# Decode through two attention and two MLP layers: unread products, two load sizes and a ring position at the end of layer 0

## The chip, the core and the metric

The kernel runs on one core of a Trainium2 chip. The metric is device time in microseconds (us) from the start of the program to its end; the profile's span is the time from the first to the last instruction. TensorE is called PE, VectorE DVE, ScalarE ACT, SyncE SP.

## The reference

Four sequences, one token each, width D = 640. Two layers with the same weights and the same caches: an attention over the last 1024 positions of 32 heads of 128, and a gated MLP of width 1728. All is float32.

```
x = x + A(layernorm(x));  x = x + B(layernorm(x))      # twice
A: q = x @ wq                        # [4, 32 heads, 128]
   p = softmax(q . k[..., -1024:, :] * 128**-0.5)
   return (p . v[..., -1024:, :]) @ wo
B: gate = x @ W_gate;  up = x @ W_up
   return (gate * (gate > 0) * up) @ W_down
```

K and V differ for each sequence and head, so each value of the caches is used for one product, and 312 MB are read from HBM in all.

## The kernel before

The heads are worked in 8 groups of 4. One DRAM tensor `stream` [128, columns] holds, in the order of use, for each group g its W_q (2560 columns), K (16384), the next group's W_q, V (16384) and W_o (2560), and behind the groups the MLP's weights: the left-over gate and up columns (1920), three gate and up blocks (5120 each), the left-over of W_down (960) and three blocks of W_down (2560 each). A column is 128 x 4 bytes.

All of it goes through one SBUF tile `store` of 55,040 columns. A list `todo` (lines 80 to 113) names the loads in order, each with its layer, its range, its largest size and, where given, its place. `load()` (line 119) takes the head of the list, places it at the cursor (`state["at"]`) or at its given place, goes back to the base when a piece no longer fits, and issues it on SP if none of its columns is live. `done()` (line 154) is called behind each product in the program's order; it frees the columns just used and calls `load()`. So a load waits on SP for the product that frees its last column, and all loads behind it wait on the same queue.

At the end of layer 0 the front of `store` is kept: layer 1 begins with group 7, whose W_q, K, V and W_o stay, together with the end of group 6's V and its W_o. What is left for streaming then is a ring of RING = 6912 columns from the column KEPT on. Through it go all MLP weights of layer 0 and, from its base again (the second `todo.append([KEPT])`, line 102), W_q of group 6 for layer 1 and the first 4096 columns of its K. After that the places of group 7's K and V come free as layer 1 uses them.

On PE each attention group is: `scores` (line 268, products `ps`, L273) with the projection of the group before after its first head, `softmax` (line 277: maximum on DVE, exponential on ACT), the next group's query, `totals` and `turned` (sums, and 8 transposes of the probabilities), and `values` (line 304: 8 blocks of 4 heads, products `po`, L309). For the last group of layer 0 there is no next query; there `table(AF.Sqrt)` loads ACT's table. The weights of V's blocks come in loads of 4096 columns (two blocks), then 2048, 1024 and 1024.

`warm()` (line 235) is a product of the identity with some tile into a PSUM buffer that nobody reads. `waits` (line 302) says after which block and head of V, in the last group of layer 0, how many of these stand: 5, 5, 2, 1 and 1, each 256 columns wide. More of them, 128 wide, stand in layer 0's MLP, `forward` (line 369): behind each fifth of the second and third gate blocks (line 385) and behind each row block of W_down's first two blocks (line 417).

`forward` computes on PE: the left-over gate columns (`gate(3)`, 15 products of 128 columns), then blocks 0, 1, 2 (20 products of 256 columns each), then `down(3)`, `down(0)`, `down(1)`, `down(2)`.

Of the kernel before, what the change touches and what calls it, by code (L numbers as in the profile page):

```python
# [12 lines left out]
B, D, H, DH, W, F = 4, 640, 32, 128, 1024, 1728  # L13
P = 128
# [9 lines left out]
WQ, KV, WO = KC * GH * P, GH * 4096, GH * D  # L24


GU0, GU = KC * 3 * P, KC * 4 * 256
WD0 = GU0 + 3 * GU
TAIL, WD1, WD = WD0 + D, WD0 + D + 2 * QUARTER, 4 * D
# [3 lines left out]
AT = {}  # L33
# [21 lines left out]
M0 = AT["mlp"]  # L55
# [12 lines left out]
def decode_kernel(ctx: ExitStack, tc: tile.TileContext, x, stream, sel, out):  # L68
# [13 lines left out]
    def run(layer, lo, hi, most=LONG, place=None):  # L82
        todo.append((layer, lo, hi, place, most))

    def steps(layer, lo, *sizes, place=None):
        for n in sizes:
            run(layer, lo, lo + n, n, place)
            lo += n
            place = None if place is None else place + n
# [8 lines left out]
    run(0, vsplit, AT["k", 7], place=0)  # L98
    steps(0, AT["k", 7], *[4096] * 7, 2048, 1024, 1024, 1280, 1280, place=FRONT + WQ)
    todo.append([KEPT])  # L100
    steps(0, M0, GU0, *[1536] * 10, WD1 - WD0, 2 * D, 3 * D, 3 * D, 2 * D, D, D)
    todo.append([KEPT])
    run(1, AT["q", 6], AT["q", 6] + WQ)
    steps(1, AT["k", 6], 2048, 2048)
    todo.append([FRONT, 0])
    steps(1, AT["k", 6] + 4096, 2560, 2048, 2048, 2048, 3584)
# [124 lines left out]
    def table(func):  # L231
        t = small.tile([P, 1], F32, name="t", bufs=1)
        nc.scalar.activation(t, eps_sb, func)

    def warm(moving=None):

        m = ident if moving is None else moving
        t = ps_p.tile([P, 512], F32, tag="p", name="unread")
        nc.tensor.matmul(t[:, :m.shape[-1]], ident, m, start=True, stop=True)  # L239
# [45 lines left out]
    def totals(sums):  # L285
        nc.tensor.matmul(ms[:, :GH * B].rearrange("p (h b) -> p h b", b=B), sums.to_broadcast([P, P]), ident_hb,  # L286
                         start=True, stop=True)
        r = small.tile([P, GH * B], F32, name="r")
        nc.vector.reciprocal(r, ms[:, :GH * B])
        return r  # L290
# [7 lines left out]
            nc.vector.tensor_copy(t[:, 4 * j:4 * j + 4], pp.rearrange("p c (b r) -> p c r b", r=32)[:, :, :GH, :])  # L298
        return t


    waits = {(1, 3): 5, (3, 3): 5, (5, 3): 2, (6, 3): 1, (7, 1): 1}

    def values(layer, g, t, last):

        for c in range(8):
            for h in range(GH):
                lo = AT["v", g] + (c * GH + h) * 512
                nc.tensor.matmul(po[32 * h:32 * h + B], t[:, c, h], get(layer, lo, 512),  # L309
                                 start=c == 0, stop=c == 7, tile_position=(0, 32 * h))  # L310
                done(layer, lo, 512)
                if last and (c, h) in waits:
                    for _ in range(waits[c, h]):
                        warm(probs[:, :256])
        nc.scalar.copy(gates, po)  # L315
        if last:
            warm(probs[:, :256])
# [18 lines left out]
    def attention(layer, gs):  # L336
        load()
        xT, d = normalized()
        rs = []
        query(layer, gs[0], xT, lambda: rs.append(deviation(d)))  # L340
        rstd = rs[0]
        table(AF.Exp)
        query_out(rstd)
        query_turned()
        before = None
        for g, after in zip(gs, gs[1:] + [None]):
            scores(layer, g, 0)
            if before is None:
                go_on()
            else:  # L350
                project(layer, before, values_turned(r), False)
            for h in range(1, GH):
                scores(layer, g, h)
            sums = softmax()
            if after is not None:
                query(layer, after, xT)
                query_out(rstd)
            else:
                table(AF.Sqrt)
            r = totals(sums)  # L360
            t = turned()
            if after is not None:
                query_turned()
            values(layer, g, t, layer == 0 and after is None)
            before = g
        project(layer, before, values_turned(r), True)


    def forward(layer):
# [38 lines left out]
        def down(j, last=False):  # L408
            for f in range(4 if j < 3 else 1):
                lo = M0 + (WD1 + j * WD + f * D if j < 3 else WD0)  # L410
                w = get(layer, lo, D)
                for g in range(4):
                    nc.tensor.matmul(y[32 * g:32 * g + B], hTs[j][:, f], w[:, g * QUARTER:(g + 1) * QUARTER],
                                     start=False, stop=last and f == 3, tile_position=(0, 32 * g))
                done(layer, lo, D)
                if layer == 0 and j < 2:
                    warm()
            if j == 3:
                w = get(layer, M0 + TAIL, 2 * QUARTER)
                for g in range(4):  # L420
                    r = slice(64 * (g // 2), 64 * (g // 2) + 64)
                    nc.tensor.matmul(y[32 * g:32 * g + B], hTs[j][r, 1], w[r, g % 2 * QUARTER:(g % 2 + 1) * QUARTER],
                                     start=False, stop=False, tile_position=(r.start, 32 * g))
                done(layer, M0 + TAIL, 2 * QUARTER)
# [80 lines left out]
```

## Time and profile before

| | us |
|---|---|
| three timed runs | 747.44, 747.61, 748.26 |
| median | 747.61 |
| the profiled execution | 748.54 |
| its span | 746.8 |
| PE busy in it | 498.0 (67%) |
| DVE busy, ACT busy | 59.3, 42.2 |

HBM was read at 418 GB/s over the span. The granted clock of PE is 0.802 of full speed in the mean. A float32 product appears as two PE records. The chain of waits follows the work that ended last back from the end; where it stands on a load, the time counted runs from that load's issue, and loads queue, so it isn't the duration of the transfer. A busy PE is counted by modelled ends of products.

### The profile page before, as it was taken

To read this page: it belongs to the slowest core of one execution; us is meant where nothing else is said; L and a number is where in the kernel's file an instruction comes from. 1 tells how busy PE (TensorE), PEld (TensorE's weight loads), DVE (VectorE), ACT (ScalarE), POOL (GpSimd) and SP (SyncE) were. 2 spreads that over 40 slices of the span, in tenths; PEclk is the share of its full clock that TensorE was granted. 3 is DMA by queue.
4 is the path that set the end of the run, shared out by engine and by line. 5 is a ranking of instruction groups with operands and counts; after the bars stand their busy time and mean duration, and the time that the engine had idled before them with its cause. 6 is when DMAs were issued, how large, how long until landed. Compare 5 with 4: busy or idle time off the path is not lost.

```text
span 746.8 us, 8319 instructions
## 1 busy us (share of the span) xinstructions
PE 498.0 (67%) x3876; PEld 167.6 (22%) x3876; DVE 59.3 (8%) x159; ACT 42.2 (6%) x74; POOL 0.2 (0%) x4
## 2 busy tenths in 40 slices
PE   3467466665855565966988997556665487576595
PEld 1122112212210121311434232111221022222142
DVE  2000100001010010101011110100001000010110
ACT  2000000000000000001001000000000000000100
POOL 0000000000000000000000000000000000000000
PEclk9969787876876776885999897868869778698777
DMA  9999999999999999999989999999999999999996
GB/s 382 454 416 433 436 429 429 436 423 440 425 438 429 437 422 425 442 412 426 374 332 390 411 447 403 412 416 444 430 442 423 442 423 435 428 430 427 412 428 282
DMA packets 14730, 312.99 MB, mean 419 GB/s; under 512 B 1636, under 2 KB 1892, under 8 KB 6120
## 3 DMA queue, kind: packets, MB, share of 16 engines
q1 hardware_dynamic: 14544, 312.37, 98.2%
q8 instruction: 30, 0.49, 0.3%
q10 hardware_dynamic: 152, 0.09, 0.0%
q14 instruction: 4, 0.03, 0.0%
HBM read 312.37 MB, written 0.08 MB: 418 GB/s over the span
## 4 chain that ended last, share of the span: by engine, by line
DMA 71%; PE 25%; another core or an unknown queue 2%; DVE 1%; ACT 1%; issue 1%; SPq 0%; ACTq 0%; DVEq 0%
DMA store<-in_stream 71%; PE ps L273 7%; PE po L309 7%; PE yy L332 3%; PE ms L321 2%; PE unread L239 1%; PE qp L253 1%; PE pp L297 1%; PE qp L381 1%; PE po L381 1%; PE ms L264 1%; DVE nm L280 0%; ACT probs L282 0%; SPq L144 0%
## 5 line engine op out<-in xcount | busy, mean ns | idle before, releaser
L273 PE MATMUL ps<-store,qz 128*4 128x512 f32 x1024 | 168.6, 719 | 100.9 <-DMA store<-in_stream 100.4
L309 PE MATMUL po<-store,pT 128*4 128x512 f32 x1024 | 165.1, 752 | 71.5 <-DMA store<-in_stream 71.5
L273 PEld LDWEIGHTS ps<-store,qz 128*4 128x4 f32 x1024 | 30.4, 97 | 208.6 <-issue 111.7
L309 PEld LDWEIGHTS po<-store,pT 128*4 128x4 f32 x1024 | 29.1, 98 | 185.5 <-issue 104.2
L253 PE MATMUL qp<-store,xT 128*4 128x512 f32 x160 | 39.3, 721 | 27.8 <-DMA store<-in_stream 27.6
L282 ACT ACTIVATE probs<-ps,nm 128x1024 f32<-128x1024 f32 x16 | 17.8, 1113 | 316.7 <-DVE nm L280 316.7
L280 DVE TENSOR_REDUCE nm<-ps 128x1 f32<-128x1024 f32 x16 | 19.6, 1225 | 196.5 <-PE ps L273 196.5
L332 PE MATMUL yy<-store,oT 128*4 128x160 f32 x512 | 27.6, 372 | 4.3 <-DVE oT L324 4.3
L324 DVE TENSOR_TENSOR oT<-ms,r 128x16 f32<-128x16 f32 x16 | 2.8, 175 | 345.7 <-PE ms L321 345.7
L315 ACT COPY gates<-po 128x512 f32<-128x512 f32 x16 | 9.4, 585 | 308.0 <-PE po L309 308.0
L321 PEld LDWEIGHTS ms<-sel_sb,gates 128*128 128x128 f32 x128 | 20.5, 244 | 20.2 <-issue 18.0
L321 PE MATMUL ms<-sel_sb,gates 128*128 128x4 f32 x128 | 21.9, 295 | 0.9 <-ACT gates L315 0.8
L297 PE MATMUL pp<-sel_sb,probs 128*128 128x128 f32 x128 | 20.9, 317 | 0.0
L381 PE MATMUL po<-store,xT 128*4 128x256 f32 x160 | 15.9, 495 | 7.0 <-DMA store<-in_stream 7.0
L297 PEld LDWEIGHTS pp<-sel_sb,probs 128*128 128x128 f32 x128 | 18.6, 178 | 0.0
L286 PE MATMUL ms<-sel_sb,sm 128*128 128x16 f32 x32 | 7.4, 308 | 15.8 <-ACT probs L282 15.7
L264 PEld LDWEIGHTS ms<-sel_sb,gates 128*128 128x128 f32 x128 | 16.8, 204 | 4.5 <-DVE gates L258 4.4
L264 PE MATMUL ms<-sel_sb,gates 128*128 128x4 f32 x128 | 16.6, 253 | 1.7 <-DVE gates L258 1.7
L253 PEld LDWEIGHTS qp<-store,xT 128*4 128x4 f32 x160 | 6.0, 93 | 50.3 <-DMA store<-in_stream 31.3
L332 PEld LDWEIGHTS yy<-store,oT 128*4 128x4 f32 x512 | 13.8, 100 | 12.1 <-DVE oT L324 5.7
L258 DVE TENSOR_SCALAR gates<-qp,rstd 128x512 f32<-128x512 f32 x16 | 12.0, 750 | 41.1 <-PE qp L253 39.8
L286 PEld LDWEIGHTS ms<-sel_sb,sm 128*128 128x128 f32 x32 | 5.8, 226 | 34.6 <-ACT probs L282 28.1
(62 smaller groups left out, 128.1 us busy)
## 6 DMA issues: line engine op xcount, KB each, us to landing
store<-in_stream SPq DMA_DIRECT2D x26, 6656.0 KB, 49.5
store<-in_stream SPq DMA_DIRECT2D x11, 2048.0 KB, 29.6
store<-in_stream SPq DMA_DIRECT2D x2, 6784.0 KB, 50.2
store<-in_stream SPq DMA_DIRECT2D x7, 1280.0 KB, 10.9
store<-in_stream SPq DMA_DIRECT2D x10, 768.0 KB, 7.1
store<-in_stream SPq DMA_DIRECT2D x7, 1024.0 KB, 8.2
store<-in_stream SPq DMA_DIRECT2D x1, 6848.0 KB, 46.8
store<-in_stream SPq DMA_DIRECT2D x1, 6720.0 KB, 46.6
```

The lines of the kernel that those rows point to most:

```text
L253: nc.tensor.matmul(qp[q:q + B], xT[:, c], get(layer, lo, GH * P), start=c < 4, stop=c > 0, tile_position=(0, q))
L258: nc.vector.tensor_scalar(gates, qp, rstd, SCALE, op0=ALU.mult, op1=ALU.mult)
L264: nc.tensor.matmul(ms[:, h * B:h * B + B], gates[:, h * P:(h + 1) * P], sel_b, start=True, stop=True)
L273: nc.tensor.matmul(ps[32 * b:32 * b + GH, j, :], qz[:, turn[0], b, GH * h:GH * h + GH], get(layer, lo, 512), start=h == 0, stop=h == GH - ...
L280: nc.vector.tensor_reduce(nm, flat, axis=AX.X, op=ALU.max, negate=True)
L282: nc.scalar.activation(probs, flat, AF.Exp, bias=nm, accum_out=sums)
L286: nc.tensor.matmul(ms[:, :GH * B].rearrange("p (h b) -> p h b", b=B), sums.to_broadcast([P, P]), ident_hb, start=True, stop=True)
L297: nc.tensor.transpose(pp[:, c, :], probs[:, (4 * j + c) * P:(4 * j + c + 1) * P], ident)
L309: nc.tensor.matmul(po[32 * h:32 * h + B], t[:, c, h], get(layer, lo, 512), start=c == 0, stop=c == 7, tile_position=(0, 32 * h))
L321: nc.tensor.matmul(ms[:, b * GH:b * GH + GH], gates[:, b * P:(b + 1) * P], ident[:, b:P:32], start=True, stop=True)
L332: nc.tensor.matmul(y[32 * q:32 * q + B], oT[:, h], get(layer, lo + q * QUARTER, QUARTER), start=False, stop=last and h == GH - 1, tile_pos ...
L381: nc.tensor.matmul(gu[32 * g:32 * g + B, :2 * n], xT[:, c], get(layer, lo, 2 * n), start=c == 0, stop=c == KC - 1, tile_position=(0, 32 * g))
```

## The change

Five edits, all at the end of layer 0 or just behind it.

1. `waits` and the 14 unread products between the last group's V blocks are taken out; the one behind the last block (line 317) stays.
2. In the same group, between the scores and the sums, two unread products of `gates` (512 columns wide) are put on PE.
3. The first MLP load, 1920 columns, becomes two of 1152 and 768. The ten pieces of 1536 behind it become 1536 x 3, 1024, 768, 1536 x 5 and 1280.
4. The cursor no longer goes back to KEPT before group 6's W_q. It goes on where the last MLP weights end, and W_q is loaded as 512, 1536 and 512 columns instead of 2560 at once.
5. The unread products behind W_down's first block are taken out; those behind its second block stay.

```diff
-    steps(0, M0, GU0, *[1536] * 10, WD1 - WD0, 2 * D, 3 * D, 3 * D, 2 * D, D, D)
-    todo.append([KEPT])
-    run(1, AT["q", 6], AT["q", 6] + WQ)
+    steps(0, M0, 9 * P, 6 * P, *[1536] * 3, 1024, 768, *[1536] * 5, 1280, WD1 - WD0, 2 * D, 3 * D, 3 * D, 2 * D, D, D)
+    steps(1, AT["q", 6], 512, 1536, 512)
...
-    waits = {(1, 3): 5, (3, 3): 5, (5, 3): 2, (6, 3): 1, (7, 1): 1}
...
-                if last and (c, h) in waits:
-                    for _ in range(waits[c, h]):
-                        warm(probs[:, :256])
...
                 table(AF.Sqrt)
+                if layer == 0:
+                    warm(gates)
+                    warm(gates)
...
-                if layer == 0 and j < 2:
+                if layer == 0 and j == 1:
                     warm()
```

## The prediction

> **What bounds the kernel now.** I read the page first: its span and the shares of the chain of waits.
>
> ```profile
> span 746.8 us, 8319 instructions
> ...
> DMA 71%; PE 25%; another core or an unknown queue 2%; DVE 1%; ACT 1%; issue 1%; SPq 0%; ACTq 0%; DVEq 0%
> ```
>
> The stream of loads sets the end; whatever changes the time must change when the loads run. So next I cut the span into stretches around the only place where the change acts, the end of layer 0. Columns: PE, PE weight loads, DVE, ACT and POOL busy time with instruction counts, then granted clock, share of the DMA engines, GB/s.
>
> ```profile
> 343.15:370.00 26.85, 24.07 (x121) 9.25 (x121) 1.93 (x4) 3.27 (x5) 0.00 (x0) 0.76 1.01 418
> 370.00:378.00 8.00, 6.92 (x134) 4.81 (x134) 1.68 (x8) 0.86 (x3) 0.00 (x0) 1.00 0.41 136
> 378.00:394.00 16.00, 12.50 (x114) 4.89 (x114) 0.86 (x4) 0.73 (x2) 0.00 (x0) 1.00 1.02 414
> 394.00:404.00 10.00, 9.27 (x132) 4.48 (x132) 0.61 (x3) 0.39 (x2) 0.00 (x0) 1.00 0.99 368
> 404.00:412.00 8.00, 6.45 (x62) 2.62 (x62) 2.17 (x8) 2.01 (x4) 0.00 (x0) 0.91 1.00 391
> 412.00:441.80 29.80, 28.28 (x250) 9.36 (x250) 3.05 (x7) 1.79 (x3) 0.00 (x0) 0.91 1.04 436
> ```
>
> From 370 to 378 us the loads move 136 GB/s where the stretch before moved 418: the stream runs dry there. Why, the chain in order of time tells (start, length, what; a product of float32 is two records).
>
> ```profile
> 343.18 3.64 PE ps L273 x16
> ...
> 349.42 0.61 PE ms L286 x2
> ...
> 351.82 3.53 PE po L309 x16
> ...
> 358.01 1.83 PE po L309 x16
> ...
> 368.28 0.98 PE po L309 x4
> ...
> 369.34 0.59 ACT gates L315
> ...
> 371.30 1.31 PE yy L332 x32
> ...
> 374.29 1.08 PE qp L381 x25
> ...
> 375.39 4.22 DMA store<-in_stream
> ```
>
> The chain is on PE from 343 to 375 us: the MLP's ring is full, and the next load waits for the first MLP products (L381, which begin at 374.29) to free its columns; it is issued at 375.39. On the way stand the unread products (a group of PE instructions from 351 to 370 us: records, busy us, mean ns):
>
> ```profile
> L239 PE MATMUL unread<-probs,sel_sb 128*128 128x256 f32 x30 | 8.4, 412 | 0.0
> ```
>
> 28 of these 30 records are the 14 products that the change takes out, 7.8 us of PE. Whether that moves anything depends on when V lands. Pairs of rows, the issue of a load (start, length) and its KB and us to landing:
>
> ```profile
> 333.34 0.33 SPq L144 DMA_DIRECT2D store<-in_stream  x1
> ...
> store<-in_stream SPq DMA_DIRECT2D x1, 512.0 KB, 29.6
> ...
> 357.87 0.33 SPq L144 DMA_DIRECT2D store<-in_stream  x1
> ...
> store<-in_stream SPq DMA_DIRECT2D x1, 768.0 KB, 14.3
> ...
> 360.37 0.33 SPq L144 DMA_DIRECT2D store<-in_stream  x1
> ...
> store<-in_stream SPq DMA_DIRECT2D x1, 768.0 KB, 13.6
> ...
> 375.39 0.33 SPq L144 DMA_DIRECT2D store<-in_stream  x1
> ...
> store<-in_stream SPq DMA_DIRECT2D x1, 768.0 KB, 4.2
> ```
>
> Following `load()` through its list gives the loads' order and names. The last 1024 columns of V land at 333.34 + 29.6 = 362.94; the last two MLP pieces that fill the ring at 357.87 + 14.3 = 372.17 and 360.37 + 13.6 = 373.97, so in a full queue 768 KB (1536 columns) are 1.80 us apart. W_o follows V with 2560 columns, 3.0 us at that rate, so by 365.9. The refill lands at 379.59 instead of 373.97 + 1.80 = 375.77. By landings the dry spell costs 3.8 us, and a load into an empty queue pays 4.2 - 1.8 = 2.4 us for starting.
>
> **The change part by part.** *The 14 products.* Without them PE waits for V's last piece, not for itself: 362.94 + 0.98 (the x4 row) = 363.9 against 369.3 now, 5.4 us sooner. W_o is there in time: 369.34 to 371.30 is 1.96 us, so the projection begins at 365.9, when W_o's last piece is landing. The first MLP products move from 374.29 to 368.9, and their weights (landing before 368.5: 372.17 less two pieces of 1.80) are in.
>
> *The first MLP load in two, and the pieces behind it.* The first refill becomes 1024 columns and is freed by eight of the fifteen 128-column products instead of twelve, 0.4 us sooner (1.08 us over the fifteen). Its issue: 375.39 - 5.4 - 0.4 = 369.6. To lose nothing it must be out 2.4 us before 373.97, so by 371.6: it is 2.0 us early. Behind it on SP stand only further loads of the ring, which wait for PE in their order; each then follows the landing of its data by under 1.5 us, while the ring holds 6912 columns, 8.1 us of stream. The dry spell goes: 3.8 us by landings, 8 x (1 - 136/418) = 5.4 us by bytes, since most engines of the sixteen are done before the slowest. PE waits for landings, so I take 4.1, near the lower.
>
> *Four more DMAs in all* (one more in the first load, one in the pieces behind it, two in W_q). Rows bound the price of each between nothing (768 KB in 1.80 us are 437 GB/s, no less than the 436 of the last stretch above, whose loads are larger) and the 2.4 us of an empty queue. I take 0.05 each, the rounding of such rows, 0.2 us in all, because the queue stays full; at the other end stand 9.6. The Trainium skill (DMA: Bandwidth & Descriptors, Anatomy of one DMA) gives every DMA about 2.0 us of fixed cost beside its bytes at 436 GB/s, by which four more would add 8 us. The trace agrees where the queue is dry (768 KB: 3.8 us by its formula as an estimate, 4.2 measured) and not where it is full (1.80).
>
> *Two unread products in the softmax.* Their width is 512; the nearest rows are the 256-wide ones, 412 ns a record, and 512-wide blocks of four tiles, 3.53 us for two at clock 0.50. So 1.8 us each at half clock, 3.5 together, into PE's idle slot from 346.8 to 349.42: up to 1.0 us over. That delays the sums and the transposes, and nothing waits for these: V's blocks 0 and 1 are in, blocks 4 and 5 come only at 357.9 (the landing for which the load of 357.87 waited). If that cover were gone it would cost 1.0. In return PE is busy without a break from 343.2. The clock changes only at the ends of stretches of 3.41 us:
>
> ```profile
> 270.67:274.09 3.42, 1.12 (x10) 0.10 (x3) 0.00 (x0) 0.00 (x0) 0.00 (x0) 0.99 0.87 369
> 274.09:277.50 3.41, 1.23 (x8) 0.26 (x12) 0.00 (x0) 0.00 (x0) 0.00 (x0) 0.50 1.12 482
> ...
> 376.49:379.90 3.41, 1.52 (x24) 0.55 (x16) 0.28 (x1) 0.01 (x1) 0.00 (x0) 1.00 0.89 337
> 379.90:383.31 3.41, 3.41 (x38) 1.53 (x34) 0.42 (x2) 0.37 (x1) 0.00 (x0) 1.00 1.03 428
> ...
> 352.59:356.01 3.42, 3.42 (x18) 0.92 (x11) 0.00 (x0) 0.00 (x0) 0.00 (x0) 0.51 0.98 407
> 356.01:359.42 3.41, 3.41 (x26) 1.74 (x24) 0.00 (x0) 0.00 (x0) 0.00 (x0) 1.00 0.98 402
> ```
>
> A full stretch raises it (356.01), 1.12 busy of 3.42 drops it (274.09), 1.52 of 3.41 keeps it. With the two products the rise comes near 349 instead of 356; V's first four blocks are then done by about 355, and PE stands until 357.9.
>
> *W_q in the ring's end; no unread products in the first block of W_down.* A step of such a product is 381.94 - 381.52 = 0.42 us:
>
> ```profile
> 380.98 0.61 PE L381 MATMUL qp<-store,xT 128*4 128x256 f32 x8
> 381.52 0.49 PE L239 MATMUL unread<-sel_sb 128*128 128x128 f32 x2
> 381.94 0.61 PE L381 MATMUL qp<-store,xT 128*4 128x256 f32 x8
> ...
> 396.50 6.91 DMA store<-in_stream
> ```
>
> Four of them free 1.7 us of PE, and these are covered: the last MLP weights come at 396.50 + 6.91 = 403.4, and PE waits for them; without that cover they would be a gain.
> W_q's 512 columns go out with those weights and 1536 a step of W_down sooner. From 394 to 412 us the stream misses 10 x (1 - 368/414) + 8 x (1 - 391/414) = 1.6 us; these edits gain between 0 and that; I take half, 0.8, since landings lose less than bytes. W_q's and the later pieces wait on SP for products of W_down, with only loads of the next K behind them, whose first reader is some 30 us away.
>
> **Sum.** 4.1 + 0.8 - 0.2 = 4.7 us. The profiled execution took 748.54 us (1.74 around its span), 0.93 above the median; 748.54 - 4.7 = 743.84, and with 0.93 off that is **742.9**. The bounds of the terms together: a gain of 3.6 to 7.0.
>
> **What is late next.** PE then runs layer 1's first group from kept weights while its own releases feed the stream, until the first K of another group goes out:
>
> ```profile
> 428.37 0.33 SPq L144 DMA_DIRECT2D store<-in_stream  x1
> ...
> store<-in_stream SPq DMA_DIRECT2D x1, 256.0 KB, 13.4
> ...
> 436.65 0.33 SPq L144 DMA_DIRECT2D store<-in_stream  x1
> ```
>
> That load leaves at 436.65, and the one before it lands at 428.37 + 13.4 = 441.8: 5.1 us ahead, 2.7 more than the 2.4 it needs. If the stream gains that much more than PE does, it is dry here.
>
> **Rivals.**
> *Hand-over takes part back (745.2).* PE's 33 us from 403.4 to 436.65 hold two or three half-clock stretches more (3.41 us, 1.7 lost in each, so 3.4 to 5.1); the slack of 2.7 less the 0.8 by which the stream gains on PE covers 1.9 of it, so 1.5 to 3.2 of the 4.7 are lost, 2.3 in the middle. For: the clock's mean there is 0.91 with waits for softmax and normalization in it, and what it is depends on where the stretches fall. Against: it needs several at once.
> *All of the bytes' deficit comes back (740.6).* 5.4 + 1.6 = 7.0, if the slowest engine is another one each time. Against: after a dry spell all engines start level, and without it the lag stays.
> *No difference (746.9).* The clock falls in the gap before 357.9, PE is late by 3 to 4 us at the first refill, and the spell shrinks by 0.7 (under 1.5). For: the row at 274.09. Against: the 2.0 us by which the refill is early.
> *Slower (749.6).* The removed products kept the clock. A stretch laid over the gap of 2.8 us holds as little as 0.6 us busy, below the 1.12 that dropped it. At half clock blocks 4 to 7 end near 366.6 (3.53 us for two blocks from 357.9, then 1.76 and two half blocks of 1.7), projection and normalization take twice as long, and the refill goes out at about 375.2, as now. The MLP's second gate block then begins cold: five steps of 0.96 us (380.98 to 381.94) twice over, 9.6 us, where its 5120 columns land in 6.0; 3.6 less some 1.6 of cover (the ring's 8.1 us less start, a piece of 1.8 and its 2.3 of work), so 2.0 us added. It decides from the point that the clock is still 0.50 when that block starts. Against: cold PE has no gaps, and a full stretch raises the clock. The Trainium skill (TensorE: Matmul & The Clock Gate, Part 1) has the clock fall after a whole idle window of about 3.4 us; by that the 2.8 us gap is safe. The row at 270.67 says less than a whole one is enough.
> *Each small DMA pays its start (752 or more).* 4 x 2.4 = 9.6 less 4.7, on 747.61. Only if the queue were dry at each; the 414 GB/s between 378 and 394 us speak against it.
>
> **How the numbers follow.** Forecast (741.2 to 744.6) 0.60, hand-over 0.13, all bytes 0.09, no difference 0.10, slower 0.06, small DMAs 0.02. About 0.2% (1.5 us) can be told from no change here. Faster 0.60 + 0.13 + 0.09 = 0.82, same 0.10, slower 0.08. The range 740.4 to 746.2 leaves out no change, both slower cases and a little of the top.
>
> **What would show it.** Right: last V product near 364, first refill issued at 369 to 371, no slice under 350 GB/s between 370 and 378, last MLP weights landing near 399. Clock: a rise near 347 to 350, and whether it stays 1.00 until the MLP. Hand-over: the load of 436.65 moves by at least 4 us. Wrong: a refill after 373, or a clock of 0.50 in the second gate block.

## The result and the profile after

The changed kernel takes 0.9935 of the time before, with a 95% interval of 0.9912 to 0.9958: medians 744.62 us against 749.95 us over 20 runs each. On the 747.61 us shown before, that is 742.7 us, 4.9 us less. Single runs of one kernel lie up to 7 us apart (741.53 to 748.30 us for the changed one), and a later section shows where part of that comes from. The profiled execution took 742.0 us.

The page of the changed kernel, its span and the shares of the chain of waits:

```profile
span 740.2 us, 8264 instructions
...
DMA 78%; PE 18%; another core or an unknown queue 2%; DVE 1%; issue 0%; SPq 0%; ACT 0%; ACTq 0%
```

The span went down by 6.6 us, and the chain stands on loads for 78% of it instead of 71%. The same stretches as those shown of before, in the changed kernel (the same columns: busy time of PE, PE weight loads, DVE, ACT and POOL, then granted clock, DMA share, GB/s):

```profile
343.15:370.00 26.85, 20.16 (x177) 7.07 (x180) 3.17 (x10) 3.57 (x6) 0.00 (x0) 0.94 1.01 416
370.00:378.00 8.00, 5.98 (x84) 2.49 (x79) 0.87 (x4) 0.94 (x3) 0.00 (x0) 1.00 0.96 346
378.00:394.00 16.00, 13.80 (x141) 5.07 (x140) 0.87 (x4) 0.74 (x2) 0.00 (x0) 1.00 1.01 401
394.00:404.00 10.00, 8.23 (x119) 3.71 (x111) 1.86 (x8) 1.52 (x3) 0.00 (x0) 1.00 1.03 402
404.00:412.00 8.00, 7.36 (x66) 2.66 (x70) 0.49 (x2) 0.52 (x2) 0.00 (x0) 1.00 1.00 406
```

The dry spell of 136 GB/s from 370 to 378 us is gone but for a remainder: 346 GB/s, with the 416 of the stretch before as the rate of a full queue. The stretches from 394 to 412 us rose from 368 and 391 to 402 and 406. The chain in order of time says what stands there now:

```profile
333.58 29.57 DMA store<-in_stream
363.19 1.05 PE po L305 x4
...
369.27 0.85 PE qp L377 x17
370.14 5.51 DMA store<-in_stream
...
392.15 7.23 DMA store<-in_stream
...
431.01 21.66 DMA store<-in_stream
```

Where before PE had the chain without a break from 343 to 375 us, a load of V issued at 333.58 now has it until it lands, and PE follows: the last V product begins at 363.19, the first MLP products at 369.27, and the first refill of the ring is out at 370.14. The last MLP weights come at 392.15 + 7.23 = 399.4 instead of 403.4.

The gain has two parts. Their rows are the issues of the two loads that follow the MLP's end, in the kernel before and in the changed one. Each pair of rows is the issue (start, length) and the load's KB with its us to landing. Before:

```profile
437.07 0.38 SPq L144 DMA_DIRECT2D store<-in_stream  x1
...
store<-in_stream SPq DMA_DIRECT2D x1, 3840.0 KB, 29.6
...
465.18 0.33 SPq L144 DMA_DIRECT2D store<-in_stream  x1
...
store<-in_stream SPq DMA_DIRECT2D x1, 6656.0 KB, 19.6
```

After:

```profile
431.43 0.39 SPq L143 DMA_DIRECT2D store<-in_stream  x1
...
store<-in_stream SPq DMA_DIRECT2D x1, 3840.0 KB, 30.4
...
458.69 0.33 SPq L143 DMA_DIRECT2D store<-in_stream  x1
...
store<-in_stream SPq DMA_DIRECT2D x1, 6656.0 KB, 18.9
```

The first holds the end of K of group 0 in layer 1, with the next W_q and the first 2048 columns of V behind it; the second, called the V load here, holds the next 13,312 columns of V. The K load lands at 437.07 + 29.6 = 466.67 before and at 461.83 after, 4.8 us sooner. The V load lands at 484.78 before and 477.59 after, 7.2 us sooner. In between, the kernel before lost 2.4 us more: its V load went out 466.67 - 465.18 = 1.49 us ahead of the landing in front of it and landed 18.1 us behind that; in the changed kernel it went out 3.14 us ahead and landed 15.8 us behind. What frees its space is a short run of PE's work, in the chain of the kernel before:

```profile
460.74 1.81 PE ms L321 x8
...
462.81 2.36 PE yy L332 x32
```

and in that of the changed one:

```profile
456.11 1.00 PE ms L314 x8
...
457.36 1.31 PE yy L325 x32
```

The same work takes nearly twice as long before: from 460.0 to 465.5 us the granted clock was 0.50 there, and from 456.1 to 458.7 us it is 1.00 in the changed kernel. From that landing to the end of the span both kernels need the same: 262.0 and 262.6 us. In the twelve experiments, where that landing could be read, the same remainder is 261.9 to 263.2. **So, to 1.3 us, all that these kernels differ in is made between V's last landing near 363 us and that landing near 480.**

### The profile page after: what moved, and what is told of

It reads as the page before. It is cut to its first block, busy times and chain, and to the rows that moved or that the text cites. A ratio compares the mean times of both kernels' runs of the same rounds, so it can differ in the third digit from the quotient of the medians.

```text
span 740.2 us, 8264 instructions
## 1 busy us (share of the span) xinstructions
PE 487.1 (66%) x3844; PEld 158.5 (21%) x3844; DVE 59.0 (8%) x159; ACT 42.2 (6%) x74; POOL 0.2 (0%) x4
## 4 chain that ended last, share of the span: by engine, by line
DMA 78%; PE 18%; another core or an unknown queue 2%; DVE 1%; issue 0%; SPq 0%; ACT 0%; ACTq 0%
DMA store<-in_stream 78%; PE ps L272 6%; PE po L305 4%; PE yy L325 2%; PE ms L314 2%; PE qp L252 1%; PE ms L263 1%; PE pp L296 0%; PE qp L377 0%; PE po L377 0%; SPq L143 0%; PE yy L409 0%; PE unread L238 0%; DVE oT L317 0%
## 5 line engine op out<-in xcount | busy, mean ns | idle before, releaser
L252 PE MATMUL qp<-store,xT 128*4 128x512 f32 x160 | 41.1, 760 | 26.7 <-DMA store<-in_stream 26.6
L325 PE MATMUL yy<-store,oT 128*4 128x160 f32 x512 | 25.5, 351 | 4.3 <-DVE oT L317 4.3
L296 PE MATMUL pp<-sel_sb,probs 128*128 128x128 f32 x128 | 19.0, 296 | 0.0
L296 PEld LDWEIGHTS pp<-sel_sb,probs 128*128 128x128 f32 x128 | 17.0, 166 | 0.0
```

What stands on the lines that cost most here:

```text
L252: nc.tensor.matmul(qp[q:q + B], xT[:, c], get(layer, lo, GH * P), start=c < 4, stop=c > 0, tile_position=(0, q))
L296: nc.tensor.transpose(pp[:, c, :], probs[:, (4 * j + c) * P:(4 * j + c + 1) * P], ident)
L325: nc.tensor.matmul(y[32 * q:32 * q + B], oT[:, h], get(layer, lo + q * QUARTER, QUARTER), start=False, stop=last and h == GH - 1, tile_pos ...
```

## The experiments

All twelve kernels compute the whole reference. Ratios are to the kernel before on the same chip, with their 95% intervals; the first four share one chip, the next four another, the last four a third. The *refill* is the first load of the MLP's ring that waits for PE.

### One part alone, one part undone

The theory is that the 14 products are nearly the whole change. **The products out, and nothing else**, in the kernel before:

```diff
-    waits = {(1, 3): 5, (3, 3): 5, (5, 3): 2, (6, 3): 1, (7, 1): 1}
...
-                if last and (c, h) in waits:
-                    for _ in range(waits[c, h]):
-                        warm(probs[:, :256])
```

> The kernel before without the 14 unread products, nothing else changed. Theory (dry spell, V's landing sets PE): the clock rises near 356 as before, blocks 0 to 3 end by 358, V's last product ends 1 us after its last piece lands, and the first refill leaves about 7 us after that landing (12.45 before, 6.96 in the changed kernel), 1.5 us before it would cost anything. The load landings keep their spacing there; 3.5 to 4.5 us faster than before. Rival (the removed products kept the clock): 0.50 between 357 and 370 in the profile, the refill leaves 11 us or more after V's last landing, within 1.5 us of before.

Measured 0.9964 [0.9946, 0.9982], 2.7 us faster. Its chain:

```profile
333.71 29.58 DMA store<-in_stream
363.34 1.05 PE po L309 x4
...
370.52 5.80 DMA store<-in_stream
```

V's end and the refill moved as they do in the changed kernel, without any other edit. The mechanism is the one predicted; what it is worth in time is less.

**The two products in the softmax, and nothing else**, in the kernel before:

```diff
                 table(AF.Sqrt)
+                if layer == 0:
+                    warm(gates)
+                    warm(gates)
```

> The kernel before with the two unread products in the softmax, nothing else changed. Theory: the clock rises near 346 to 350 instead of 356, so that V's blocks 0 to 3 and the ten products between them run at full clock; PE is at V's end about 366 instead of 369.3, the refill leaves 9 to 10 us after V's last landing, 0.5 to 1 us too late: 2.5 to 3.5 us faster than before. Rival (the 14 products alone are what stood in the way): the refill is as late as before, 12 us behind the landing, and the time within 1 us of before.

Measured 0.9979 [0.9960, 0.9998], 1.6 us faster. In its profile the clock is up from 341.8 us on, 3 us before the first of the two products begins (345.0), V's first four blocks are done when the landing of 357.9 comes, and the blocks behind it follow at once, with the unread products still between them:

```profile
357.94 1.90 PE po L309 x16
359.84 1.06 PE unread L239 x4
```

The refill goes out 9.29 us behind V's last landing, against 12.45 before and 6.96 in the changed kernel.

**The 14 products put back** into the changed kernel, all else as changed:

```diff
+    waits = {(1, 3): 5, (3, 3): 5, (5, 3): 2, (6, 3): 1, (7, 1): 1}
...
+                if last and (c, h) in waits:
+                    for _ in range(waits[c, h]):
+                        warm(probs[:, :256])
```

> The changed kernel with the 14 unread products put back. Theory: with the early clock they cost PE 2.1 us at V's end, not 5.4; the refill leaves near 9 us after V's last landing, 0.2 to 0.6 us too late: at most 1 us slower than the changed kernel, 3.5 to 4.5 faster than before. Rival (the 14 products are the whole dry spell): 4 us slower than the changed kernel, within 1 us of before.

Measured 1.0006 [0.9985, 1.0026]: nothing left of the gain, where my theory had most of it stay, since by the 2.4 us taken for enough the refill would be late by tenths. It did go out where expected; pairs of rows, the last load that fills the ring and the refill:

```profile
362.22 0.33 SPq L143 DMA_DIRECT2D store<-in_stream  x1
...
store<-in_stream SPq DMA_DIRECT2D x1, 768.0 KB, 12.5
...
372.96 0.33 SPq L143 DMA_DIRECT2D store<-in_stream  x1
...
store<-in_stream SPq DMA_DIRECT2D x1, 512.0 KB, 3.6
```

It left 362.22 + 12.5 - 372.96 = 1.76 us ahead of the landing in front of it and landed at 376.56, 1.84 us behind that, for 1.24 us worth of bytes in the changed kernel (its refill of the same size lands at 375.64, behind one at 374.40). The stream says the same, and that the loss isn't over there; the clock is at half until 405.5 us as well (two of the stretches):

```profile
370.00:378.00 8.00, 7.61 (x112) 4.63 (x116) 1.51 (x7) 1.10 (x4) 0.00 (x0) 0.79 0.73 256
...
404.00:412.00 8.00, 6.32 (x83) 3.33 (x86) 2.17 (x8) 2.04 (x4) 0.00 (x0) 0.91 0.83 280
```

So being out before the landing isn't enough. This is the first step of the prediction that fell.

**The softmax's two products taken out** of the changed kernel:

```diff
-                if layer == 0:
-                    warm(gates)
-                    warm(gates)
```

> The changed kernel without the two unread products in the softmax. Theory: the clock rises near 356, V's first four blocks are done by 358 at the latest, V's end and the refill are as in the changed kernel within 0.5 us (7 us after V's last landing), the time within 0.7 us of it, 4 to 5 faster than before. Rival (without the pair the clock stays down through V): 0.50 after 358, refill 10 us or more after the landing, 2 to 4 us slower than the changed kernel.

Measured 0.9969 [0.9949, 0.9988]. Against 0.9953 and 0.9935 of the changed kernel in its two measurements that is 1.2 to 2.5 us slower, and all three intervals overlap: the runs can't say that the pair is worth nothing, nor that it is worth 2 us.

### The loads

**The changed kernel again**, for the chip of the next three:

> The changed kernel once more, to be timed beside its own variants. Ratio to the kernel before 0.992 to 0.996 (0.9935 so far).

Measured 0.9953 [0.9930, 0.9975], 3.5 us faster than before. The two measurements agree within their intervals.

**The MLP's loads as they were** (no extra DMA), all else as changed:

```diff
-    steps(0, M0, 9 * P, 6 * P, *[1536] * 3, 1024, 768, *[1536] * 5, 1280, WD1 - WD0, 2 * D, 3 * D, 3 * D, 2 * D, D, D)
+    steps(0, M0, GU0, *[1536] * 10, WD1 - WD0, 2 * D, 3 * D, 3 * D, 2 * D, D, D)
```

> The changed kernel with the MLP's loads as before (1920, then 1536 each); W_q goes on behind them. Theory (a load loses the less the earlier it is out: over the six profiles so far loads out 1 to 2 us before the previous landing cost 1.4 us over their bytes, 2 to 3 us 0.6, 3 to 4 us 0.37, 4 to 5 us 0.33, 5 to 6 us 0.2, more 0.13): the first refill leaves 7.2 us after V's last landing instead of 7.0, all margins in the MLP are smaller by 0.2 to 0.5 us, 0 to 0.8 us slower than the changed kernel. Rival (only a load less than 2.4 us ahead costs anything): no difference, since none is.

Measured 0.9974 [0.9949, 0.9999].

**W_q again from the ring's base in one load**, all else as changed:

```diff
-    steps(1, AT["q", 6], 512, 1536, 512)
+    todo.append([KEPT])
+    run(1, AT["q", 6], AT["q", 6] + WQ)
```

> The changed kernel with W_q of group 6 from the ring's base in one load of 2560, as before. Theory (margins): that load leaves a step of W_down or two later, about 3 us ahead of the previous landing instead of 5 to 6, and the K behind it too: 0.3 to 1.0 us slower than the changed kernel, last MLP weights landing unchanged, the first K of the next group 0.3 to 1 us later. Rival (threshold of 2.4 us): no difference. Should W_q be what carried the gain: 3 us or more slower.

Measured 0.9975 [0.9954, 0.9995].

**Smaller loads still**, five DMAs more than the changed kernel (16 pieces instead of 11 behind the MLP's first two loads; the expectation below counts four):

```diff
-    steps(0, M0, 9 * P, 6 * P, *[1536] * 3, 1024, 768, *[1536] * 5, 1280, WD1 - WD0, 2 * D, 3 * D, 3 * D, 2 * D, D, D)
-    steps(1, AT["q", 6], 512, 1536, 512)
+    steps(0, M0, 9 * P, 6 * P, *[1024] * 4, 768, *[1024] * 6, 768, *[1024] * 3, 512, WD1 - WD0, 3 * D, 2 * D, 3 * D, 2 * D, D, D)
+    steps(1, AT["q", 6], 1024, 1024, 512)
```

> The changed kernel with smaller MLP loads: 1152, 768, 1024 x 4, 768, 1024 x 6, 768, 1024 x 3, 512, W_down's pieces so ordered that the ring is full (1920, 1280, 1920, 1280, 640, 640), W_q as 1024, 1024, 512: four DMAs more. Theory (margins): refills leave about 0.6 us earlier, the margins in the MLP rise from 4 to 5 us to about 5, each load loses 0.05 to 0.1 less, the four more DMAs give it back: within 0.7 us of the changed kernel. Rival (a fixed 2 us for each DMA): 8 us slower.

Measured 0.9975 [0.9954, 0.9997], and a span of 743.7 us in the profile. The second profile of the changed kernel has that span too, but with a lower clock in W_down, as a table below shows, so it is the times that count. All three kernels are 1.6 us above that kernel's ratio, inside the intervals. The last one settles the rival by which each small DMA pays its start: five more would be 5 x 2.4 = 12 us, and even the far ends of the two intervals (0.9997 and 0.9930) are only 5.0 us apart. Its stream shows no trace of it:

```profile
370.00:378.00 8.00, 5.37 (x84) 1.83 (x77) 0.80 (x4) 0.94 (x3) 0.00 (x0) 1.00 1.00 379
```

That is the smallest dent of all profiles there, 379 GB/s against 346 in the changed kernel. By the rule of the Trainium skill (DMA: Bandwidth & Descriptors, Anatomy of one DMA) of about 2.0 us fixed for each DMA, five more would add, as an estimate, 10 us; neither the time nor this row agrees, as long as the loads stand in a queue. That section fits its figure to DMAs that GpSimd issues, and all loads here are issued on SP, so the case doesn't test the fit itself.

**Larger loads**: the refills in pieces of 2304 columns.

```diff
-    steps(0, M0, 9 * P, 6 * P, *[1536] * 3, 1024, 768, *[1536] * 5, 1280, WD1 - WD0, 2 * D, 3 * D, 3 * D, 2 * D, D, D)
+    steps(0, M0, 9 * P, 6 * P, 2560, *[2304] * 5, 1280, WD1 - WD0, 2 * D, 3 * D, 3 * D, 2 * D, D, D)
```

> The changed kernel with larger MLP pieces: 1152, 768, 2560, then 2304 each, 1280 (three DMAs fewer). A refill is out 0.9 us later, and the ring holds three pieces instead of four and a half. Theory (what counts is how far ahead of the previous landing a load is out): margins in the MLP fall from 4 to 5 us to 2 to 3.5, each of its six or seven large loads loses 0.3 to 0.8 us more: 2 to 4 us slower than the changed kernel. Rival (threshold of 2.4 us): under 1 us slower.

Measured 0.9991 [0.9968, 1.0014], 2.8 us above the changed kernel's 0.9953 (the intervals just overlap), and 281 GB/s from 370 to 378 us. With fewer DMAs, but each issued later (a large piece needs a large space to come free), the gain is lost. That fits a size that counts by how far ahead a load can be issued, and not by a price for each. How much of the 2.8 us the loads cost themselves, and how much the clock in W_down, which is low in this profile too, one profile doesn't say.

Each load issued between 300 and 480 us, in all fourteen profiles, can be set against the landing in front of it: how far ahead of that landing it was issued, and how much longer it needed behind that landing than its bytes take at 427 KB a us (768 KB in 1.80 us, as the prediction shows). That rate is a little too high, so an undisturbed load shows 0.1 us here. 523 loads have both landings in the trace. There is a second thing that can make a load late: packets of 16 KB on a queue that brings instructions to the engines (the last section shows its row). The table parts the loads by whether such a packet was running between 1 us before the landing in front and the load's own landing:

| issued so far ahead of the landing in front | no such packet: loads, mean excess, over 0.3 us | packet: loads, mean excess, over 0.3 us |
|---|---|---|
| under 1 us, or behind it | 1, 1.87 us, 1 | 1, 3.79 us, 1 |
| 1 to 2 us | 6, 0.95 us, 6 | 2, 1.92 us, 2 |
| 2 to 3 us | 15, 0.45 us, 10 | 2, 1.30 us, 2 |
| 3 to 4 us | 46, 0.36 us, 13 | 11, 0.73 us, 7 |
| 4 to 5 us | 41, 0.10 us, 1 | 17, 1.05 us, 15 |
| 5 to 6 us | 61, 0.08 us, 0 | 16, 0.47 us, 6 |
| over 6 us | 194, 0.09 us, 0 | 110, 0.24 us, 23 |

A lag can carry over from one load to the next, so a row isn't the price of its loads alone; but the trend is plain. Without a packet, every load issued less than 2 us ahead was late, most at 2 to 3 us, about one in four at 3 to 4 us, and of the 296 issued 4 us or more ahead a single one. So a load has to be out some 4 us before its predecessor lands to cost no more than its bytes. The prediction had 2.4, read from one load into an empty queue. What loads with a longer lead still lose goes along with the packets: 44 of 143 are late by over 0.3 us. That is a correlation over the profiles; no run sets a load's lead or a packet alone.

### Products behind W_down, and the late edits without the early one

**The unread products behind W_down's first block put back**, all else as changed:

```diff
-                if layer == 0 and j == 1:
+                if layer == 0 and j < 2:
```

> The changed kernel with the four unread products behind W_down's first block put back. Theory: they lie in PE's wait for the last MLP weights; the refills behind that block leave up to 1.7 us later (W_q's 1536 columns 3.5 us ahead of the previous landing instead of 5), so 0 to 0.6 us slower than the changed kernel. Rival (they held W_q back): 1.5 us slower or more, and the first K of the next group leaves 1.5 us later.

Measured 0.9963 [0.9939, 0.9987], 0.7 us above 0.9953: covered, as predicted, as far as the intervals tell.

**Edits 3 to 5 alone**, in the kernel before (the unread products between V's blocks as before, none in the softmax):

```diff
-    steps(0, M0, GU0, *[1536] * 10, WD1 - WD0, 2 * D, 3 * D, 3 * D, 2 * D, D, D)
-    todo.append([KEPT])
-    run(1, AT["q", 6], AT["q", 6] + WQ)
+    steps(0, M0, 9 * P, 6 * P, *[1536] * 3, 1024, 768, *[1536] * 5, 1280, WD1 - WD0, 2 * D, 3 * D, 3 * D, 2 * D, D, D)
+    steps(1, AT["q", 6], 512, 1536, 512)
...
-                if layer == 0 and j < 2:
+                if layer == 0 and j == 1:
```

> The kernel before with the MLP's and W_q's part of the change alone: loads in two and smaller pieces, W_q in the ring's end, no unread products in W_down's first block; the 14 products stay in V and there is no pair in the softmax. Theory (the gain is made ahead of the MLP): the first refill leaves 12.0 us after V's last landing (12.45 before), the landings there lose 3 to 3.5 us as before, and the whole is 0 to 1 us faster than before. Rival (the loads and W_q carry half of the gain): 2.5 us faster.

Measured 1.0037 [1.0019, 1.0055]: 2.8 us *slower* than before, clear of its interval and against both theories. Stretches of 3.41 us of its profile, laid where its clock changes:

```profile
380.49:383.90 3.41, 1.56 (x14) 0.50 (x14) 0.00 (x0) 0.00 (x0) 0.00 (x0) 1.00 0.97 383
383.90:387.31 3.41, 2.81 (x13) 0.87 (x14) 0.00 (x0) 0.00 (x0) 0.00 (x0) 0.50 1.02 414
...
397.59:401.00 3.41, 0.79 (x17) 0.46 (x17) 0.00 (x0) 0.00 (x0) 0.00 (x0) 1.00 0.89 358
401.00:404.40 3.40, 2.63 (x20) 1.06 (x21) 0.17 (x1) 0.00 (x0) 0.00 (x0) 0.50 1.00 400
```

Its first three refills go out only 0.7, 3.3 and 3.4 us ahead, since PE is as late as before, so their weights come late; PE waits for them, and a stretch with 1.56 and one with 0.79 us of work drop the clock to 0.50, twice in the MLP. At half clock PE frees the ring later, and the next loads are later again. In the kernel before the clock stays at 1.00 until 410.6 us. This is one profile, and it holds three edits at once: which of them costs isn't parted.

### The clock in the changed kernel's own profiles

The question is therefore at which times the clock changes. The two profiles of the changed kernel itself differ by 3.5 us of span, 740.2 and 743.7. Stretches between the points at which a change can fall, first of the profile with 740.2:

```profile
356.74:360.15 3.41, 1.90 (x16) 0.36 (x16) 0.00 (x0) 0.00 (x0) 0.00 (x0) 1.00 0.99 402
...
390.87:394.28 3.41, 1.82 (x42) 0.81 (x41) 0.09 (x1) 0.00 (x0) 0.00 (x0) 1.00 1.03 402
394.28:397.70 3.42, 2.87 (x39) 1.35 (x39) 0.17 (x1) 0.00 (x0) 0.00 (x0) 1.00 0.99 381
```

then of the one with 743.7:

```profile
394.48:397.90 3.42, 1.79 (x27) 0.87 (x27) 0.17 (x1) 0.00 (x0) 0.00 (x0) 1.00 0.99 399
397.90:401.31 3.41, 3.38 (x28) 1.34 (x28) 0.00 (x0) 0.00 (x0) 0.00 (x0) 0.50 1.05 411
```

In the second, a wait for the weights of W_down leaves 1.79 us of work in one stretch, the clock falls for the next, W_down runs at half speed, and the load that was out at 431.01 is out 2.8 us later (counted from V's last landing in each). The drop isn't all of that. Up to a landing 21.0 us behind V's last, the two profiles land their loads within 0.1 us of each other; then the load issued 17.0 us behind it takes 0.8 us over its bytes in the first and 1.8 in the second, and one issued some 8 us later 0.1 against 0.8. So the last MLP weights come 1.7 us later (38.0 against 36.2 us). They are issued at 393.7, ahead of the drop, so 1.7 of the 2.8 us aren't the drop's; the other 1.1 are made behind it. The kernel is the same: what differs is which loads are held up, and where the waits fall in the grid of stretches. The kernel with W_q in one load (745.6 us) shows a third place of the grid:

```profile
354.99:358.40 3.41, 0.47 (x8) 0.00 (x0) 0.00 (x0) 0.00 (x0) 0.00 (x0) 1.00 0.97 404
358.40:361.81 3.41, 3.22 (x16) 0.59 (x20) 0.00 (x0) 0.00 (x0) 0.00 (x0) 0.50 1.01 411
...
365.23:368.64 3.41, 2.58 (x42) 1.98 (x42) 0.45 (x2) 0.34 (x2) 0.00 (x0) 1.00 1.02 413
368.64:372.05 3.41, 3.36 (x59) 2.57 (x62) 0.79 (x5) 0.00 (x0) 0.00 (x0) 0.50 0.82 333
```

Here the gap before 357.9 us falls into one stretch, 0.47 us busy, and the clock does drop, as one of the rivals had it; but one stretch of V's blocks raises it again. It drops again in projection and normalization (368.64) and in W_down (395.9). All profiles side by side (the last row's kernel comes below), times counted from V's last landing (362.9 to 363.6 us in each); "drops" are those from 346 to 409 us, "W_down" is the granted clock from 397 to 405 us, "K" the issue of the load of 431.01, "V" the landing of that of 458.69:

| kernel | refill out | drops at (us) | W_down | K out | V lands | span |
|---|---|---|---|---|---|---|
| before | 12.45 | none | 1.00 | 73.7 | 121.8 | 746.8 |
| changed | 6.96 | none | 1.00 | 67.8 | 114.4 | 740.2 |
| changed, again | 6.98 | 397.9 | 0.79 | 70.6 | 117.4 | 743.7 |
| products out alone | 7.21 | 350.0, 387.5, 408.0 | 1.00 | 71.2 | 120.1 | 745.4 |
| pair alone | 9.29 | 369.1 | 1.00 | 67.8 | 117.7 | 742.5 |
| products put back | 9.46 | 371.4, 398.7 | 0.60 | 75.2 | 121.8 | 748.0 |
| without the pair | 7.59 | 348.3, 358.5, 368.8, 396.1 | 0.63 | 72.9 | 119.3 | 745.5 |
| MLP loads as before | 7.22 | 357.5 | 1.00 | 68.5 | 116.7 | 741.6 |
| W_q as before | 7.81 | 358.4, 368.6, 395.9 | 0.64 | 70.2 | 119.3 | 745.6 |
| smaller loads | 6.97 | none | 1.00 | 67.5 | not read | 743.7 |
| larger loads | 9.71 | 357.5, 371.2, 398.5 | 0.59 | 75.3 | 121.5 | 747.7 |
| W_down's products back | 7.82 | 358.2, 368.4 | 1.00 | 66.9 | 116.2 | 742.0 |
| edits 3 to 5 alone | 10.42 | 349.8, 383.9, 401.0 | 0.75 | 76.7 | 123.9 | 749.5 |
| projection earlier | 7.59 | 358.7, 369.0, 396.3 | 0.62 | 72.9 | 119.0 | 744.3 |

Among the kernels that differ from the changed one in a single point and have their refill out by 7.9, the clock in W_down parts them: where it stayed up, K is out at 66.9 to 68.5, where it fell, at 70.2 to 72.9, without overlap, 4 us apart in the middle. W_down's column doesn't tell all, though: the products out alone have 1.00 there and K at 71.2. The table stops at 409 us, and the clock drops again behind that. Counted from 390 us to K's issue, the stretches at half clock add up to 0 or 3.4 us in the five profiles with K at 66.9 to 68.5, and to 6.8 to 13.7 us in all nine others. What one of them costs can be read from the last MLP weights to K's issue. PE needs 30.0 us there without such a stretch (the pair alone, W_down's products back), 31.6 to 31.7 with one (changed, MLP loads as before, smaller loads) and 33.2 with two (before: the drops at 410.6 and 424.2). So each costs about 1.6 us, and one fewer of them is 1.6 of the 5.9 us by which K moved between the profiles before and after; the rest, 4.3, is the earlier landing of the weights.

That is one profile of each kernel, and a correlation. It isn't tried by a run that moves the grid alone, and I know of none that would.

### The next late load

The prediction named the load of 436.65, the first K, as late next. The profiles show the V load behind it instead (465.18 before): it waits for the projection of layer 1's second group, which stands behind the first head of the next group's scores, and these wait for that K. **The projection moved ahead of those scores**, in the changed kernel:

```diff
-            else:
+            elif not (layer == 1 and g == 0):
                 project(layer, before, values_turned(r), False)
...
             before = g
+            if layer == 1 and g == 6:
+                project(layer, before, values_turned(r), False)
```

> The changed kernel, where in layer 1 group 6 is projected right behind its V instead of behind the first scores of group 0: the same instructions, two steps of PE exchanged. PE waits there for group 0's K in any case (451.6 to 457.6 us in the kernel before), and the load of V that follows waits for that W_o's columns. In the profiles so far that load was out 1.5 to 3.2 us ahead of the previous landing and lost 0 to 2.5 us over its bytes (mean 1.5 over seven). Theory (margins): it leaves 4 us or more sooner, loses under 0.3 us; 0.4 to 2 us faster than the changed kernel. Rival (the stream makes it up later, or the next load of that place waits on something else): no difference.

Measured 0.9943 [0.9921, 0.9965], 0.7 us below 0.9953: it can't be told from the changed kernel. The load did what was meant; its issue and landing:

```profile
456.66 0.33 SPq L143 DMA_DIRECT2D store<-in_stream  x1
...
store<-in_stream SPq DMA_DIRECT2D x1, 6656.0 KB, 25.6
```

The end of K lands at 466.50 here. The V load is out 466.50 - 456.66 = 9.8 us ahead of it instead of 3.14, and lands 15.76 us behind it, which is its bytes. But the changed kernel's profile with 740.2 already had 15.76 there, and this profile had three clock drops before (358.7, 369.0, 396.3), with K out at 72.9. What the edit takes away is a loss that comes only in some executions: of the profiles, V's load cost 2.5 us over its bytes in the kernel before, 2.3, 1.5 and 1.3 in three others, and 0.4 to 0.6 in three. That the time over many runs goes down by it isn't shown.

## Why the prediction was right, and where it wasn't

**The time.** Forecast 742.9, measured 742.7 by the ratio; the sum of 4.7 us stands against 4.9 [3.1, 6.6], and 3.5 [1.9, 5.2] in the second measurement. The agreement with the first is closer than the measurement allows to claim, and part of it is luck: the sum has no term for the half-clock stretches behind 403 us, and the profiles differ by them (below).

**The 14 products: right.** V's end was put at 363.9 and came at 363.19 + 1.05 = 364.24; the refill at 369.6, and it came at 370.14; the last MLP weights near 399, and they came at 399.4. Taken alone the edit moves the refill by 5.2 of the 5.5 us, and gains 2.7 us of the 4.1.

**The dry spell: the term was right, its threshold wrong.** Left in the bytes are 8 x (1 - 346/416) = 1.35 us of the 5.4, so 4.0 came back where 4.1 was taken. By landings all 3.8 came back: the refill lands at 370.14 + 5.51 = 375.65, 1.25 us behind the load in front, and its 512 KB take 1.20. But "to lose nothing it must be out 2.4 us before" failed. The 2.4 was the start of a load into an empty queue, and a load issued 2 to 3 us ahead still cost 0.45 us over its bytes in the mean, with no packet of instructions near it, one issued 3 to 4 us ahead 0.36, and only from 4 us on the 0.1 of an undisturbed load. The refill at 4.26 us ahead wasn't "2.0 us early" but about as late as it may be. That is also why "no slice under 350 GB/s between 370 and 378" did not hold (the mean of all eight is 346): engines that are done early stand idle without a landing being later for it. And it is part of why the kernel with the 14 products back, with 1.76 us of lead, kept none of the gain: its last MLP weights come 3.4 us later than in the changed kernel (39.6 against 36.2 us behind V's last landing). The other 4.0 us by which its K is later come behind them, with four half-clock stretches of 3.41 us instead of one between 390 us and K.

**Four more DMAs: right** in that they cost little; the smaller loads show it with five more. But I had them only as a price. Their use, that a small piece is freed and issued sooner, decides: larger pieces gave 2.8 us back, with a low clock in W_down beside it.

**The pair in the softmax: the rise was luck, its worth missing.** The clock was to rise near 349; it rose at 346.5, and then stayed up until 412. But the pair begins only at 346.73, so the scores raised it, and with the 14 products out alone, without the pair, it rose at 346.6 too. What the pair does is keep it up. The stretch over the softmax holds 2.66 us of PE's work with the pair (346.46 in the changed kernel) and 0.75 without it (346.56, the products out alone). In the three profiles without the pair whose clock was up, it fell behind that stretch (348.3, 349.8, 350.0); in none of the ten with the pair did it fall there. The price was put at nothing, and the gain too: alone it gains 1.6 us [0.15, 3.0], and in its profile the refill goes out 3.2 us sooner, V's first blocks being done at full clock; that profile's clock had risen before the pair, at 341.8, so how much of the 1.6 is the pair's and how much the grid's isn't shown. With the 14 products gone that gain is mostly theirs already, and what is left couldn't be separated.

**W_q and W_down: a bound was wrong.** These edits were to gain "between 0 and 1.6". In the changed kernel 394 to 412 us recovered 10 x (402 - 368)/414 + 8 x (406 - 391)/414 = 1.1 us, inside the bounds; alone, with the MLP's loads, they cost 2.8 us. The lower bound of nothing supposed a clock of 1.00 in the MLP, and the sum that the terms are independent. They aren't: in that run's one profile PE is late, waits for its weights, and the waits drop its clock.

**What is late next: wrong load.** The load of 436.65 moved to 431.01, by 5.6 us, and lost nothing, so the hand-over rival didn't come. Its price for a half-clock stretch was right (1.7 put, 1.6 read), but the profile after has one stretch fewer between the last weights and that load, not several more; no edit sets that. In other profiles such stretches did take part back: without the pair there are four, the last weights come 1.5 us later than in the changed kernel, and K 5.1 us later. The one that mattered was the next, at 465.18. In the profile before it lost 2.5 us, which the prediction didn't follow. There the small products and the projection (rows above) ran at half clock before and at full clock after, so 2.4 of the profile's 6.6 us came with a clock that no edit sets: in other profiles of this study they ran at half clock again (the smaller loads, 1.81 and 2.36 us).

**The clock rivals.** The drop in the gap before 357.9 is real: it comes in six of the ten profiles without the 14 products, whenever the grid lays a whole stretch over it (0.3 to 1.0 us busy). I gave it too little chance, and its price was over-rated: one stretch of V's blocks raises the clock, and the refill is 0.3 to 0.9 us later, not 5. The place where drops cost is another, from W_down to K's issue, some 40 us later; of the rivals only the hand-over named it, and that only from 403.4 us on. The rule of the Trainium skill (TensorE: Matmul & The Clock Gate, Part 1) that the clock falls after a whole idle window would have kept it up at all of these places. The trace disagrees: stretches with 1.56 and 1.79 us busy of 3.41 dropped it, and no length of busy time parts the two cases, since 1.52 (the row of 376.49 in the prediction), 1.82 and 1.90 kept it. That the windows run freely, as the same section has it, agrees: changes within a profile lie whole multiples of 3.41 us apart (346.7 and 397.9, 15 of them), and start elsewhere in each.

## What to carry to other kernels

A load in a full queue costs its bytes only if it is issued well before the one in front of it lands (4 us here, not the 2.4 us that one load into an empty queue lost): size the pieces of a ring so that the first space that comes free is already worth a load, and judge an edit by each load's lead, not by whether the queue is empty. Follow the loads past the place of the change until their lead is the same in both kernels; only there is the difference closed. And where a waiting engine has a clock that falls, an edit that shortens its work isn't free even off the chain, so look for the stretch that it leaves too thin. Two profiles of one kernel differ by 3.5 us here, so take more than one before explaining 3 us.

## What the hardware showed that I hadn't expected

**Busy time alone doesn't hold the clock.** Stretches of many small products dropped it with far more busy time than those that kept it above: 2.58 us of 3.41 in the row of 365.23 (projection and normalization, 42 records), and 2.29 before the drop at 410.6 in the kernel before. What counts as work for the clock is therefore not the busy column; its measure stays open.

**Data comes late where code is loaded.** The page of the changed kernel shows a queue that moves instructions:

```profile
q8 instruction: 30, 0.49, 0.3%
```

Each is a packet of 16 KB that takes about 1.1 us (median of the 30 in each of the fourteen profiles). One comes between 380 and 385 us in every kernel, and the load in flight there lands late in most: in the two profiles of the changed kernel the one issued at 380.2 and 380.6 with 4.0 us of lead took 0.8 and 1.8 us over its bytes, while its neighbours with 4.7 to 5.7 took none; in the kernel before a load with 5.6 us of lead took 1.5. Over all profiles the table of leads says it: of the loads issued 4 us or more ahead, 44 of 143 with such a packet near their landing were late by over 0.3 us, and 1 of 296 without. The Trainium skill (Runtime: NRT & Kernel Launch, Instruction fetch mechanics) gives 16 KiB blocks and calls the cost of crossing into the next mostly hidden; the size agrees, and these landings speak against hidden for the data loads; whether an engine waited for its instructions isn't read here. That the packet is the cause wasn't tried by a run.
